# Routed attention into a gated MLP on one core: centroid constants in two PSUM banks, tanh and gate over 512 columns, and a new order

## The chip, the cores and the metric

The program runs on one core of a Trainium2 chip. The core has a matrix engine (PE), whose weight loads are shown apart (PEld), a vector engine (DVE), a scalar engine for activation functions (ACT), a general engine (POOL), and SP, which here issues DMAs. Each engine takes its own instructions in order, and engines wait for each other through semaphores. PE writes to PSUM, which has eight banks of 128 partitions x 512 fp32 values; POOL and DMAs can't reach it. The metric is the device time of one launch in microseconds (us), lower is better.

## The reference

Attention in which a query sees only the keys that have the same nearest centroid, then an MLP with w_in, SiLU and w_out. B, H, S, D = 4, 8, 768, 64; 16 centroids for each head; 3072 tokens, model width 512, hidden width 2048.

```python
q_assign = np.argmax(np.einsum('bhsd,hcd->bhsc', q_n, c_n), axis=-1)   # q_n, k_n, c_n: rows of length 1
k_assign = np.argmax(np.einsum('bhsd,hcd->bhsc', k_n, c_n), axis=-1)
mask = q_assign[:, :, :, None] == k_assign[:, :, None, :]
scores = scale * np.matmul(q, k.transpose(0, 1, 3, 2))
scores = np.where(mask, scores, -1000000000.0)
attn = np.exp(scores - np.max(scores, axis=-1, keepdims=True))
attn = attn / (np.sum(attn, axis=-1, keepdims=True) + 1e-09)
x = np.matmul(attn, v)                        # to [B * S, H * D]
h = x @ w_in
out = (h * (1.0 / (1.0 + np.exp(-h)))) @ w_out
```

## The kernel before

`build` describes the work as a graph of some 1,900 steps. A step has a list of engines that may do it, the steps it comes after, and the buffers that it uses (`POOLS`: so many tiles of a name; `M` are the eight PSUM banks). What sets the order is the string `PLAN`: it holds the buffer number for every buffer, and then the steps in the order in which they are recorded, each with the engine chosen for it. Every engine thus runs its steps in the plan's order. Entries below zero are filler matmuls on zeros (L951), which use PE while it would have nothing to do; there are 43.

The stages, with the letters that end a step's tag:

- **Centroids.** Loaded, scaled to length 1, split in an fp16 high and low part (`c_split`), transposed on PE (`c_turn`, L330) and copied to `st2` (`c_place2`, two steps, one for the high part and one for the low) and `stk` (`c_place`). `st2` holds the constants with which the first batch's logits are made.
- **Tokens of a pair of heads.** A pair p of heads of batch b has one buffer `ab`. For the first 8 of 12 token tiles of batch 0 (`part2`): an fp32 transpose of two tiles at once on PE (L579), a *split* on ACT (`hi`, L594), a *residual* on DVE (`lo`, L599), a *move* of the second tile's half to partitions 0 to 63, and the logits on PE (L624 to 626). For the last 4 tiles of batch 0 (`part`, tags that end in .8, such as p0.3.0.8 for pair 3) and for all tiles of the later batches: a split (L452 to 456) and a residual (L459) first, then a transposing DMA from SP (L517), then logits against `stk` (L529 and 530, or L532).
- **Codes** (`codes`): DVE finds the maximum of 16 logits, marks it and *flips* the marks (L436); four *puts* copy them to partitions 64 to 95 of `ab`, on POOL, DVE or ACT, or as a DMA on SP (L390). So the scores of different clusters fall far below those of equal ones.
- **Attention** (`attention`): scores of 128 x 512 (L685), exponential on ACT to a tile `P` (L688), product with the values (L713; the values are loaded at L257 and *cast* to `vt`), reciprocal and normalisation on DVE, a transpose (L770, in batch 0) and a *settle* to `xt`.
- **MLP** (`mlp`): unit by unit of tokens (`UNITS`: batch 0 has one of 256 tokens and one of 512, the rest have 384). For each of the 16 blocks of hidden width: four up-projections (L801) to a bank, tanh on ACT (L809), gate on DVE (L812), then the down-projections (L828), the copy out and the store. The first L801 needs all four pairs' `xt` for the first 256 tokens and the first weights, which POOL casts.

From the first L801 on, the plan mixes attention of the later batches with the MLP of the earlier ones.

Of the kernel before, what the change touches and what calls it, by code (L numbers as in the profile page):

```python
# [25 lines left out]
    "11543XvaUa;<08X8W*vvspm({+9jHIiazwtnnkkNf5nk&?iyp>(J@a+%_i5zs8%TrcSts4^|Y{weeZ43*}M&!mD2no=3a?r4yn=N*jx(y&wjafjU"
    "2n;uFckmvp8&K5U|(Bnke-4Enr6k{oPB=#GuV_$L?p)?s33mRMbRk*w&duya{%9ll)m~1~F!Tyo^$=#F{*HO&)q#=*7O59YGrf@%A}!W>11<7t+|"
    "7hD_`@X7{wSAv4m;rJxy~Xe&*?+||p$h<Uc+E@<W*WAfg$^(Ee9jl=W8rs~AlxJb4!lW5*2Y<65#Bdx6_VY7Q)#JT3WsM&>(jlGD8&sg(s*UZ<;f"
    "{@u&=b=3b{Ld~%Y_C_jV{Dwbe)c(bH&W|()aGDnop<~^5BT*t*3Z@l8Jb$H!)8yy_IXiTQ<LoZkYM&M?2nDo<L!UMRP2DMJTd02bY<%E!)67&EOt"
    "zO25c4a)+lP{=o-~ZCfMp6XXmW=k1;Fe%`3@N)u4IPklBl{t%TmXI(|gQnf&y2FWzLeYi1iV@t<1rBmUF8=#84l4%=u?G^2uk74z~zRX3eoy@*+*"  # L30
    "poxKGf5%*VYDR3$NZq%nf3A3IovL9wK6U5A{+<QR`#EN<Tw6r~{(M4yZn}Q122I>~wb84t0UJ$Wd-ssNvt#ZZ_2=pOaS`(8oBDm>`e#zW_DB40fq"
    "=g{5kKx9)TgN3-H4rU(9c%KKQ%%o2fU1R{V$Q!tPR^cy4LI6$Myg5><3>h4^Ew^&9JDyN)hvP?|UZVf87Kg`o0R<xp<Yv^`G_d8l`@Xr0%P0=NPp"
    "66SVOYuzT<Ab?SH4|Ig)+UFU#Zv4CB%kd2JgJq-KbLJzVx=)aNc$8GAl5cT6I<iGoalRs?VB*EmFW8P42kdl(<)V8aqI#>ttz%;J9pW@n#ah!T4s"
    "~qRQl%UfBt!uuH0?s|g)W@C<8KEV##-9Og0Qq2r-Nh8HeG6>`ZD2e!H2LK?qs^C+<1~VaTt5SC3+-Txxi-dm4s8rgpglA*^}%tPqR*fmpgHygbS$"
    "KYPS6>YuQOo}Jk6NyXcx!{yI?oWf=n<DI>Jhr4f~)6b9x)y3vXi2K@Y%O_yFF4LofjH!n-gJ4#E(49zK(gP1ujlhi_pZ427Mr0P@2mcn|(f2{}E{"
# [952 lines left out]
```

## Time and profile before

| | us |
|---|---|
| median of 3 runs | 301.54 (300.48 to 303.38) |
| the profiled execution | 301.66 |
| its span, first to last instruction | 299.9 |
| PE busy in it | 291.2 |
| DVE, ACT, POOL busy | 213.9, 222.6, 89.6 |

A line of a profile's group reads: source line, engine, operation, what it writes and reads, shape, count; then busy time and the mean of one in ns; then the engine's idle time just before and what ended it. A line of the timeline reads: start and length in us, engine, line, operation, count, and in brackets the idle time before it. Durations of instructions that follow each other overlap a little. The clock granted to PE is 0.998 of the full one.

### The profile page before, as it was taken

What the parts mean: (1) busy time and instruction counts of PE and PEld (TensorE: products, weight loads), DVE (VectorE), ACT (ScalarE), POOL (GpSimd) and SP (SyncE); (2) the same over time, 40 slices, a digit from 0 to 9 for tenths busy, and PEclk for the clock granted to TensorE, in tenths of its full rate; (3) what the DMA queues carried; (4) which work ended last, traced back from release to release, by engine and by line L of the source; (5) the groups of instructions that cost most, each with busy time, mean ns of one, the idle gap of its engine ahead of it and who ended that gap; (6) DMA issues with size and microseconds to landing.
All of it is one profiled execution on the core that took longest, in us unless ns stands there. A gap on an engine that the chain in (4) does not pass through costs nothing.

```text
span 299.9 us, 7820 instructions
## 1 busy us (share of the span) xinstructions
PE 291.2 (97%) x3044; PEld 187.0 (62%) x3044; DVE 213.9 (71%) x512; ACT 222.6 (74%) x456; POOL 89.6 (30%) x151
## 2 busy tenths in 40 slices
PE   7898999999999999999999999999999999999995
PEld 5776898645555676766656566566665655554553
DVE  5999988878898999889999686676552323465140
ACT  2898999888669898998888867889988732343221
POOL 3787776443655406040833212100200000000000
PEclk9999999999999999999999999999999999999999
...
GB/s 203 263 227 291 218 262 348 116 281 293 249 283 243 232 245 215 224 202 300 124 170 126 134 144 196 149 5 3 66 2 26 28 32 67 0 93 49 1 107 105
DMA packets 83382, 47.42 MB, mean 158 GB/s; under 512 B 60688, under 2 KB 78352, under 8 KB 83344
## 3 DMA queue, kind: packets, MB, share of 16 engines
...
q10 hardware_dynamic: 144, 0.03, 0.1%
...
## 4 chain that ended last, share of the span: by engine, by line
PE 83%; DVE 10%; ACT 2%; issue 2%; DMA 1%; POOL 1%; SPq 0%; DVEq 0%
PE M L801 26%; PE M L828 26%; PE M L685 17%; PE M L713 10%; DVE hl L459 3%; PE M L532 2%; DMA nat<-in_q_dram 1%; DVE gq L812 1%; DVE lo L599 1%; DVE ab L191 1%; DVE ohT L436 1%; POOL ab L191 1%; DVE oh L429 1%; DVE mx L419 1%; DVE M L422 1%
## 5 line engine op out<-in xcount | busy, mean ns | idle before, releaser
L688 ACT ACTIVATE P<-M 128x512 f16<-128x512 f32 x288 | 155.8, 622 | 18.6 <-PE M L685 17.9
L812 DVE SCALAR_TENSOR_TENSOR gq<-tn,M 128x384 f16<-128x384 f32 (+2 forms) x128 | 66.7, 548 | 47.9 <-ACT tn L809 46.4
L801 PE MATMUL M<-xt,win_s 128*128 128x384 f16 (+2 forms) x512 | 95.7, 325 | 0.0
L828 PE MATMUL M<-wout_s,gq 128*128 128x512 f16 (+2 forms) x400 | 94.8, 370 | 0.0
L685 PE MATMUL M<-ab 96*128 96x256 f16 (+1 forms) x432 | 90.5, 308 | 1.4 <-DVE ab L191 0.9
L809 ACT ACTIVATE tn<-M 128x384 f32<-128x384 f32 (+2 forms) x128 | 61.2, 512 | 36.5 <-PE M L801 32.4
L801 PEld LDWEIGHTS <-win_s 128*128 128x128 f16 x512 | 48.7, 97 | 33.5 <-issue 0.2
L828 PEld LDWEIGHTS <-gq 128*128 128x128 f16 x400 | 37.4, 97 | 36.2 <-issue 0.4
L191 POOL COPY ab<-ohT 32x384 f16<-32x384 f16 (+2 forms) x69 | 38.4, 557 | 55.6 <-DVE ohT L436 31.2
L713 PEld LDWEIGHTS <-P 128*128 128x128 f16 x1152 | 45.7, 97 | 10.5 <-issue 0.7
L713 PE MATMUL M<-vt,P 128*128 128x65 f16 x1152 | 49.2, 193 | 0.3 <-DVE oh L429 0.2
L685 PEld LDWEIGHTS <-ab 96*128 96x128 f16 x432 | 38.0, 97 | 18.3 <-DVE ab L191 0.7
L459 DVE SCALAR_TENSOR_TENSOR hl<-nat,hl 128x768 f16<-128x768 f32 (+1 forms) x28 | 29.6, 1073 | 0.1
L191 POOL CAST vt<-nv 128x384 f16<-128x384 f32 x19 | 11.3, 607 | 32.5 <-DMA nv<-in_v_dram 21.3
L456 POOL TENSOR_SCALAR hl<-nat 128x768 f16<-128x768 f32 (+1 forms) x19 | 15.1, 804 | 19.4 <-DMA nat<-in_k_dram 14.2
L436 DVE STREAM_TRANSPOSE ohT<-oh 128x384 f16<-128x384 f16 (+2 forms) x33 | 18.3, 557 | 1.0
L401 DVE TENSOR_REDUCE M<-M 128x192 f32<-128x384 f32 x24 | 13.4, 559 | 6.1 <-PE M L532 4.4
L189 ACT COPY ot<-M 128x512 f32<-128x512 f32 (+2 forms) x14 | 7.8, 558 | 12.0 <-PE M L828 12.0
L191 DVE COPY ot<-M 128x512 f32<-128x512 f32 x11 | 7.6, 687 | 8.9 <-PE M L828 8.9
L429 DVE TENSOR_SCALAR oh<-M 128x96 f16<-128x96 f32 (+4 forms) x62 | 13.1, 252 | 0.7
L743 DVE TENSOR_TENSOR xn<-M,rz 128x384 f16<-128x384 f32 x24 | 13.1, 551 | 0.7 <-DVE rz L732 0.3
L732 DVE RECIPROCAL rz<-M 128x6 f32<-128x6 f32 (+1 forms) x36 | 6.6, 182 | 8.3 <-PE M L713 8.1
...
## 6 DMA issues: line engine op xcount, KB each, us to landing
nv<-in_v_dram SPq DMA_DIRECT2D x16, 384.0 KB, 5.1
...
nat<-in_k_dram SPq DMA_DIRECT2D x15, 384.0 KB, 4.7
nat<-in_q_dram SPq DMA_DIRECT2D x12, 384.0 KB, 4.8
...
```

What stands on the lines that cost most here:

```text
L191: eng(en).tensor_copy(out, in_)
L429: e.nc.vector.tensor_scalar(out=T(oh)[:, 0:n, 0:HC].rearrange("p (g i) c -> p g i c", g=groups)[:, :, i0:i1, :], in0=from_().rearrange("p ...
L436: e.nc.vector.transpose(T(ohT)[:, 0:n, :].rearrange("p n c -> p (n c)"), T(oh)[:, 0:n, :].rearrange("p n c -> p (n c)"))
L456: e.nc.gpsimd.tensor_scalar(out=dh(), in0=src(), scalar1=QS, scalar2=1.0, op0=ALU.mult, op1=ALU.mult)
L459: e.nc.vector.scalar_tensor_tensor(out=dl(), in0=src(), scalar=QS, in1=dh(), op0=ALU.mult, op1=ALU.subtract)
L685: e.nc.tensor.matmul(bank(sb)[:, at : at + 128 * (c - a)], ab[0:96, kt[m], :], q, start=True, stop=True)
L688: e.nc.scalar.activation(out=T(P)[:, 0:n], in_=bank(sb)[:, 0:n], func=AF.Exp, bias=0.0, scale=ESC)
L713: e.nc.tensor.matmul(bank(O)[:, at : at + D + 1], T(P)[:, c : c + 128], T(vb)[:, VW * m : VW * m + D + 1], start=(m == 0), stop=(m == NJ - ...
L801: e.nc.tensor.matmul(bank(bk)[:, 0:n], e.win_s[:, r, ts(fb, 128)], T(X)[:, r, 128 * j0 : 128 * j1], start=(r == 0), stop=(r == NR - 1),)
L809: e.nc.scalar.activation(out=T(tn)[:, 0:n], in_=bank(bk)[:, 0:n], func=AF.Tanh, bias=0.0, scale=1.0)
L812: e.nc.vector.scalar_tensor_tensor(out=gq(fb // 4)[:, fb % 4, 0:n], in0=T(tn)[:, 0:n], scalar=1.0, in1=bank(bk)[:, 0:n], op0=ALU.add, op1= ...
L828: e.nc.tensor.matmul(bank(bk)[:, 0 : c1 - c0], gq(quarter)[:, fc % 4, ts(t, 128)], e.wout_s[:, fc, c0:c1], start=(fc == 0), stop=(fc == NF ...
```

## The change

- `c_turn` does two transposes, one for each part, to two banks (`pcs`), each to partitions 0 to 63. `c_place2` is cut by heads: the first pair's constants of both parts first (`s_pair`, which the first pair's logits wait for), then the other six heads (`s_others`, which the rest waits for).
- In `mlp`, units of 256 tokens put two hidden blocks side by side in one bank, and one tanh and one gate of 512 columns serve both.
- 21 tiles `P` instead of 19; `mx`, `oh` and `ohT` have 16 instead of 24 rows of codes, as none needs more. `EARLY` is gone; it was empty.
- A new `PLAN`: other engines for some steps (18 puts on SP before, 30 now; the moves of batch 0 all on POOL before, now five on POOL, two on ACT and one on SP), and another order on all engines.

```diff
-    pc = buf("M", 64)
+    pcs = [buf("M", 64), buf("M", 64)]
 
     def c_turn(_):
-        e.nc.tensor.transpose(bank16(pc)[:, 0:128], e.chl.rearrange("p a d -> p (a d)"), e.ident)
+        for part, pc in enumerate(pcs):
+            e.nc.tensor.transpose(bank16(pc)[0:64, 0:128], e.chl[:, part, :], e.ident)
...
-    def c_place2(part):
+    def c_place2(part, h0, h1):
...
-                copy(
-                    en, e.st2[64 * s : 64 * s + 64, part, :, HC * s : HC * s + HC],
-                    bank16(pc)[64 * part : 64 * part + 64, 0:128].rearrange("d (h c) -> d h c", c=HC),
-                )
+                copy(en, e.st2[64 * s : 64 * s + 64, part, h0:h1, HC * s : HC * s + HC], turned_c(part)[:, h0:h1])
...
-        s_log = step("PE", logits, after=[s_hi, s_lo, s_cent2], use=[A, lo2, Lb], kind="mm", size=(3 * w, 32), tag=tag + "l", key=key + 1)
+        s_log = step("PE", logits, after=[s_hi, s_lo, s_others if p else s_pair], use=[A, lo2, Lb], kind="mm", size=(3 * w, 32), tag=tag + "l", key=key + 1)
...
-        for fb in range(NFB):
-            bk, tn = buf("M", n), buf("tn")
+        per = 512 // n if n <= 256 else 1
+        for f0 in range(0, NFB, per):
+            bk, tn = buf("M", n * per), buf("tn")
...
             def tanh(_, bk=bk, tn=tn):
-                e.nc.scalar.activation(out=T(tn)[:, 0:n], in_=bank(bk)[:, 0:n], func=AF.Tanh, bias=0.0, scale=1.0)
+                e.nc.scalar.activation(out=T(tn)[:, 0 : n * per], in_=bank(bk)[:, 0 : n * per], func=AF.Tanh, bias=0.0, scale=1.0)
```

What the new plan moves is seen at three places. The first is the start, on ACT, from the first split (L594) to the first exponential (L688). `st2` are the constants, `ab0` is pair 0's buffer, `ohT` the flipped marks. Before:

```order
L594 ACTIVATE ab0_87<-M0_151 128x512
L189 COPY st2_68<-M1_152 64x8x16 x2
L594 ACTIVATE ab0_87<-M2_153 128x512
L594 ACTIVATE ab1_88<-M4_155 128x512
L594 ACTIVATE ab1_88<-M6_157 128x512
L189 COPY ab0_87<-ohT0_140 32x8x32 x3
L189 COPY ab0_87<-ohT1_141 32x8x32
L594 ACTIVATE ab2_89<-M7_158 128x512
L594 ACTIVATE ab2_89<-M0_151 128x512
L688 ACTIVATE P0_102<-M5_156 128x512
```

Now:

```order
L596 ACTIVATE ab0_87<-M0_153 128x512
L188 COPY st2_69<-M1_154 64x2x16 x2
L188 COPY st2_69<-M2_155 64x2x16 x2
L596 ACTIVATE ab0_87<-M3_156 128x512
L188 COPY ab0_87<-ab0_87 64x512
L188 COPY st2_69<-M2_155 64x6x16 x2
L188 COPY st2_69<-M1_154 64x6x16 x2
L596 ACTIVATE ab1_88<-M6_159 128x512
L596 ACTIVATE ab1_88<-M7_160 128x512
L188 COPY ab1_88<-ab1_88 64x512
L188 COPY ab0_87<-ohT0_142 32x8x32
L188 COPY ab0_87<-ohT1_143 32x8x32
```

All constants of `st2` are ACT's now, and two moves; the two splits into `ab2` (a third pair) moved behind the first exponential, and two of four puts to POOL. On DVE at the same place, from the split of p0.0.0.8 on, before:

```order
L454 TENSOR_SCALAR hl0_82<-nat0_76 128x8x64
L191 COPY st2_68<-M1_152 64x8x16 x2
L599 SCALAR_TENSOR_TENSOR lo20_85<-M0_151,ab0_87 128x512
L459 SCALAR_TENSOR_TENSOR hl0_82<-nat0_76,hl0_82 128x8x64
L419 TENSOR_REDUCE mx0_135<-M3_154 128x8
```

Now:

```order
L456 TENSOR_SCALAR hl0_82<-nat0_76 128x8x64
L461 SCALAR_TENSOR_TENSOR hl0_82<-nat0_76,hl0_82 128x8x64
L601 SCALAR_TENSOR_TENSOR lo20_85<-M0_153,ab0_87 128x512
L601 SCALAR_TENSOR_TENSOR lo21_86<-M3_156,ab0_87 128x512
L421 TENSOR_REDUCE mx0_137<-M4_157 128x8
```

The two constant copies left DVE, and the residual into `hl0` (what the transposing DMA reads) moved ahead of the one into `lo20` (what the first logits read).

The second place is SP's queue between the transposing DMA of p0.1.0.8 (to `ab2`) and that of batch 1's second part (to `ab4`). `nv` are values, `gq` the landing place of weights. Before:

```order
L517 DMA_TRANSPOSE ab2_89<-hl2_84 128x8x128
L257 DMA nv1_81<-in_v_dram 128x2x384
L257 DMA nv0_80<-in_v_dram 128x2x384
L282 DMA gq1_122<-in_moe_w_in_dram 128x4x256
L517 DMA_TRANSPOSE ab1_88<-hl1_83 128x8x128
L282 DMA gq2_123<-in_moe_w_in_dram 128x4x256
L517 DMA_TRANSPOSE ab4_91<-hl0_82 128x12x128
L282 DMA gq3_124<-in_moe_w_in_dram 128x4x256
L282 DMA gq4_125<-in_moe_w_in_dram 128x4x256
```

Now:

```order
L519 DMA_TRANSPOSE ab2_89<-hl0_82 128x8x128
L281 DMA gq0_123<-in_moe_w_in_dram 128x4x256
L392 DMA ab3_90<-ohT1_143 32x16x32
L519 DMA_TRANSPOSE ab1_88<-hl2_84 128x8x128
L256 DMA nv1_81<-in_v_dram 128x2x384
L281 DMA gq1_124<-in_moe_w_in_dram 128x4x256
L281 DMA gq2_125<-in_moe_w_in_dram 128x4x256
L519 DMA_TRANSPOSE ab4_91<-hl1_83 128x12x128
L281 DMA gq3_126<-in_moe_w_in_dram 128x4x256
```

The values of pair 2 (the second `nv` before, the only one now) and the weights moved behind the transposing DMA of p0.3.0.8 (to `ab1`), and a put came into the queue ahead of it. What that DMA waits for is DVE's residual into its `hl`. On DVE before it, before:

```order
L436 STREAM_TRANSPOSE ohT1_141<-oh0_138 128x256
L436 STREAM_TRANSPOSE ohT0_140<-oh1_139 128x512
L191 COPY ab3_90<-ohT0_140 32x16x32 x4
L459 SCALAR_TENSOR_TENSOR hl1_83<-nat1_77,hl1_83 128x8x64
L459 SCALAR_TENSOR_TENSOR hl0_82<-nat0_76,hl0_82 128x12x64
```

Now:

```order
L438 STREAM_TRANSPOSE ohT1_143<-oh0_140 128x512
L461 SCALAR_TENSOR_TENSOR hl2_84<-nat1_77,hl2_84 128x8x64
L438 STREAM_TRANSPOSE ohT0_142<-oh1_141 128x256
L190 COPY ab3_90<-ohT1_143 32x16x32
L190 COPY ab3_90<-ohT0_142 32x8x32
L190 COPY ab3_90<-ohT1_143 32x16x32 x2
```

The residual of p0.3.0.8 (the one of 128x8x64) moved ahead of a flip and of the puts into `ab3`.

The third place is ACT where the 256-token unit begins. Before:

```order
L809 ACTIVATE tn0_142<-M5_156 128x256
L688 ACTIVATE P2_104<-M4_155 128x512
L809 ACTIVATE tn1_143<-M6_157 128x256
L809 ACTIVATE tn2_144<-M7_158 128x256
L688 ACTIVATE P3_105<-M1_152 128x512
```

Now:

```order
L813 ACTIVATE tn0_144<-M6_159 128x512
L813 ACTIVATE tn1_145<-M4_157 128x512
L690 ACTIVATE P14_116<-M2_155 128x512
L690 ACTIVATE P7_109<-M7_160 128x512
L690 ACTIVATE P8_110<-M5_158 128x512
```

One tanh now stands where two stood, with exponentials moved between them.

More of the change, by code (lines that the diff above doesn't have):

```diff
@@ L26 @@
[L26 to L35, printed above, removed]
@@ L91 @@
 PAIRED = 6
-EARLY = {}
 CHUNK = 8
@@ L102 @@
     "vt": (10, [128, 6 * 72], f16),
-    "P": (19, [128, 512], f16),
+    "P": (21, [128, 512], f16),
     "gq": (8, [128, 2048], f16),
@@ L106 @@
     "xn": (3, [128, 6, 128], f16),
-    "mx": (3, [128, 24], f32),
-    "oh": (2, [128, 24, 32], f16),
-    "ohT": (2, [128, 24, 32], f16),
+    "mx": (3, [128, 16], f32),
+    "oh": (2, [128, 16, 32], f16),
+    "ohT": (2, [128, 16, 32], f16),
     "tn": (3, [128, 512], f32),
@@ L355, in build @@
     s = step("POOL", c_root, after=[s, s_ident], kind="const", size=520, tag="croot")
[L356 to L361 removed]
+    s = step("DVE", c_split, after=[s], kind="const", size=950, tag="csplit")
+    s = step("PE", c_turn, after=[s, s_ident], use=pcs, kind="mm", size=(2, 128), tag="cturn")
+    s_pair = [
+        step("DVE ACT", c_place2(part, 0, 2), after=[s, s_const2], use=[pcs[part]], kind="place2", size=300, tag="cplace2")
+        for part in range(2)
+    ]
+    s_others = [
+        step("DVE ACT", c_place2(part, 2, H), after=[s, s_pair[part]], use=[pcs[part]], kind="place2", size=430, tag="cplace3")
+        for part in range(2)
+    ]
+    s_cent = step("DVE", c_place, after=[s, s_const, s_others], use=pcs, kind="const", size=690, tag="cplace")
     abuf, ready = {}, {}
@@ L812, in gate @@
+            def gate(_, f0=f0, bk=bk, tn=tn):
                 e.nc.vector.scalar_tensor_tensor(
-                    out=gq(fb // 4)[:, fb % 4, 0:n], in0=T(tn)[:, 0:n], scalar=1.0, in1=bank(bk)[:, 0:n],
-                    op0=ALU.add, op1=ALU.mult,
-                )
-            y = step("ACT", tanh, after=[s], use=[bk, tn], kind="T", size=n, tag=tag + "T", key=key + fb)
-            gates.append(step("DVE", gate, after=[s, y], use=[bk, tn, g4], kind="G", size=n, tag=tag + "G", key=key + fb))
+                    out=gq(f0 // 4)[:, f0 % 4 : f0 % 4 + per, 0:n], in0=T(tn)[:, 0 : n * per].rearrange("p (f c) -> p f c", c=n),
+                    scalar=1.0, in1=bank(bk)[:, 0 : n * per].rearrange("p (f c) -> p f c", c=n), op0=ALU.add, op1=ALU.mult,
+                )
@@ L819, in mlp @@
+            y = step("ACT", tanh, after=ups, use=[bk, tn], kind="T", size=n * per, tag=tag + "T", key=key + f0)
+            s = step("DVE", gate, after=[ups, y], use=[bk, tn, g4], kind="G", size=n * per, tag=tag + "G", key=key + f0)
+            gates.extend([s] * per)
         for t in range(j1 - j0):
@@ L926 @@
     e.wout_s = const.tile([128, NFB, DM], f16, name="wout_s")
+    e.half = const.tile([128, 1], f32, name="half")
     e.ident = const.tile([128, 128], f16, name="ident")
@@ L930 @@
     e.st2 = const.tile([128, 2, H, 2 * HC], f16, name="st2")
-    e.half = const.tile([128, 1], f32, name="half")
     e.zeros = const.tile([128, 256], f16, name="zeros")
```

137 lines of the change are left out of this document (70 added, 67 removed).

## The prediction

> **What bounds the kernel now.** I read the page first: the busy shares, then the chain.
>
> ```profile
> span 299.9 us, 7820 instructions
> PE 291.2 (97%) x3044; PEld 187.0 (62%) x3044; DVE 213.9 (71%) x512; ACT 222.6 (74%) x456; POOL 89.6 (30%) x151
> ...
> PE 83%; DVE 10%; ACT 2%; issue 2%; DMA 1%; POOL 1%; SPq 0%; DVEq 0%
> ```
>
> PE is the bound: 97% busy and 83% of the chain. DVE and ACT are busy 71 and 74% and hold little of the chain. So the question is where PE is not busy. Busy time by stretch answers it (columns: length, then busy time of PE, PEld, DVE, ACT, POOL, clock, DMA share, GB/s).
>
> ```profile
> 0.00:10.00 10.00, 7.97 (x65) 5.96 (x66) 6.45 (x22) 3.60 (x6) 3.85 (x23) 1.00 0.73 218
> 10.00:20.00 10.00, 9.11 (x135) 8.00 (x134) 9.58 (x27) 9.67 (x20) 8.17 (x19) 1.00 1.04 266
> 20.00:30.00 10.00, 8.42 (x156) 7.16 (x152) 9.84 (x25) 9.17 (x20) 7.92 (x14) 1.00 1.09 254
> 30.00:40.00 10.00, 9.72 (x173) 8.55 (x173) 9.42 (x34) 9.75 (x21) 7.50 (x10) 1.00 1.03 245
> 40.00:50.00 10.00, 10.00 (x155) 8.98 (x154) 8.46 (x27) 10.00 (x27) 6.71 (x11) 1.00 1.15 296
> 50.00:60.00 10.00, 9.43 (x129) 7.27 (x127) 8.24 (x22) 9.16 (x21) 5.70 (x7) 1.00 0.57 167
> 100.00:150.00 50.00, 50.00 (x600) 32.77 (x599) 45.88 (x108) 45.75 (x94) 17.77 (x26) 1.00 0.96 220
> 290.00:300.00 10.00, 6.80 (x45) 3.70 (x43) 0.69 (x1) 1.30 (x3) 0.00 (x0) 0.95 0.26 96
> ```
>
> PE idles 2.03, 0.89, 1.58 and 0.28 us in the four stretches up to 40, 0.57 us at 50 to 60, and 3.1 us at the end, where the last output tile is copied and stored. Between 100 and 150 it idles not at all. Up to 40 DVE is at 94 to 98% from 10 on and ACT at 92 to 98%: they feed PE. From the first up-projection on, PE has MLP work for every hole:
>
> ```profile
> 37.82 0.46 PE L532 MATMUL M<-stk,ab 128*128 128x32 f16 x12
> 38.63 1.47 PE L801 MATMUL M<-xt,win_s 128*128 128x256 f16 x12
> L951 PE MATMUL M<-zeros 128*128 128x256 f16 x43 | 7.9, 327 | 1.1 <-DVE zeros L196 1.1
> ```
>
> So a gain has to make the first L801 come before 38.63, or close the 0.57 us hole. All PE idle before 60 is 5.35 us, and the 43 filler matmuls (L951) are 7.9 us of busy time that is no work; both plans hold 43 of them. More than some 5 us isn't there to be won.
>
> **The change part by part.** The sum is made against the profiled execution, 301.66 us (span 299.9 and 1.8 around it), 0.12 above the median of 301.54.
>
> *Centroid constants (start).* Rows of the start, then groups kept apart by shape:
>
> ```profile
> 6.67 0.44 DVE L191 COPY st<-M 64x128 f16<-64x128 f16 x2
> 7.13 0.69 DVE L599 SCALAR_TENSOR_TENSOR lo<-M,ab 128x512 f16<-128x512 f32 x1
> 7.20 0.53 ACT L189 COPY st<-M 64x128 f16<-64x128 f16 x2 [1.49 <-DVE st L191]
> 8.45 1.33 SPq L517 DMA_TRANSPOSE ab<-hl  x1
> 12.53 1.08 ACT L594 ACTIVATE ab<-M 128x512 f16<-128x512 f32 x2
> 13.50 2.09 ACT L688 ACTIVATE P<-M 128x512 f16<-128x512 f32 x4
> ```
>
> ACT waits 1.49 us for DVE's half of the constants, and DVE, whose next work follows at once (7.13), spends 0.44 us on them. Now ACT does all eight copies (four of 2 heads, four of 6 heads) from two banks. At most 8 x 0.265 = 2.1 us (each like the 64x128 copy); a small copy is not free, so I take 1.7. ACT has 6.4 us idle in the first 10, which hides them and the two moves of 64x512 that it also takes over (estimated at 0.6 us each, since a 512-column ACTIVATE of the row at 12.53 takes 0.54). DVE loses 0.44 us. The second transpose is one matmul more in a place of fillers (7.9 / 43 = 0.18 us each): 0 to 0.2 us, and I take 0. The residual of p0.0.0.8 now stands ahead of the one of p0.0.0.0 on DVE: the transposing DMA (8.45) is issued about 1 us earlier, and the first logits end about 0.3 us later (0.69 more, 0.44 less ahead of their residual), which eats part of the 0.44. The first exponential, at 13.50 behind two splits (12.53, 1.08 us), comes to about 12.4, because those two splits now stand behind it; that is an exchange on ACT, worth 0.1 us.
>
> *Up to the first up-projection.* The settle that releases L801 is DVE's. Ahead of it DVE now has two constant copies, one cast, one flip of 256 and two puts of 512 columns fewer, and two splits (512 and 768 columns) more:
>
> ```profile
> L191 DVE CAST vt<-nv 128x384 f16<-128x384 f32 x11 | 4.4, 402 | 0.0
> L436 DVE STREAM_TRANSPOSE ohT<-oh 128x256 f16<-128x256 f16 x6 | 2.6, 438 | 0.2
> L191 DVE COPY ab<-ohT 32x512 f16<-32x512 f16 x6 | 3.0, 502 | 0.1
> L454 DVE TENSOR_SCALAR hl<-nat 128x512 f16<-128x512 f32 x1 | 0.8, 845 | 0.5 <-DMA nat<-in_q_dram 0.5
> L454 DVE TENSOR_SCALAR hl<-nat 128x768 f16<-128x768 f32 x7 | 4.4, 644 | 0.7 <-DMA nat<-in_k_dram 0.6
> 16.43 12.04 ACT L688 ACTIVATE P<-M 128x512 f16<-128x512 f32 x24
> 29.30 3.54 ACT L688 ACTIVATE P<-M 128x512 f16<-128x512 f32 x7 [0.83 <-PE M L685]
> ```
>
> -0.44 - 0.40 - 0.44 - 1.00 + 0.85 + 0.64 = -0.8 us. ACT, with 48 exponentials ahead of the first tanh instead of 47 and the same four splits since the first scores, allows between -0.1 us (its hole of 0.83 stays) and -0.9 (it closes). I take DVE's 0.8, as DVE is the fuller one. The twelve logits at 37.82 (0.46 us with the last one's drain, which overlaps; I take 0.3) stood ahead of the first L801 and now stand behind it, so 0.5 us of PE time is won: **-0.5**, bounds -0.9 (no logits to make up for) and +0.3 (the first logits' delay comes through and nothing else).
>
> *Tanh and gate of 512 columns.*
>
> ```profile
> 39.77 0.55 ACT L809 ACTIVATE tn<-M 128x256 f32<-128x256 f32 x1
> 40.04 0.78 ACT L688 ACTIVATE P<-M 128x512 f16<-128x512 f32 x1
> L812 DVE SCALAR_TENSOR_TENSOR gq<-tn,M 128x512 f16<-128x512 f32 x16 | 10.3, 673 | 2.2 <-ACT tn L809 2.2
> L812 DVE SCALAR_TENSOR_TENSOR gq<-tn,M 128x256 f16<-128x256 f32 x16 | 6.4, 414 | 1.7 <-ACT tn L809 1.3 <-issue 0.2
> ```
>
> The next ACTIVATE starts 0.27 us after a 256-column tanh, and 512 columns follow each other every 12.04 / 24 = 0.50 us: 16 x 0.27 - 8 x 0.50 = 0.3 us off ACT. DVE saves 16 x 0.414 - 8 x 0.673 = 1.2 us. But PE is 10.00 of 10.00 busy at 40 to 50, where these stand: its own backlog hides both, **0**; were that cover gone, ACT's 0.3 would count. The Trainium skill, "ScalarE: Activation LUTs" (What ACT_TABLE_LOAD costs), gives 186 ns + 0.833 ns a column with about 93 ns of overlap, so an estimate from that page is 8 x 92 ns = 0.7 us; the trace's 0.3 is less. If ACT set the end there, the sum would be 300.2 by the page and 300.6 by the trace.
>
> *The hole at 56.*
>
> ```profile
> 53.60 1.83 DVE L459 SCALAR_TENSOR_TENSOR hl<-nat,hl 128x768 f16<-128x768 f32 x1
> 53.59 2.75 POOL L191 CAST wout_s<-gq 128x1024 f16<-128x1024 f32 x2
> L459 DVE SCALAR_TENSOR_TENSOR hl<-nat,hl 128x768 f16<-128x768 f32 x24 | 26.7, 1129 | 0.1
> 56.05 0.28 PE L770 MATMUL M<-ident,xn 128*128 128x128 f16 x2 [0.57 <-DVE xn L737]
> ```
>
> PE waits 0.57 us for a normalisation that DVE does behind a residual of 1.83 us, 0.7 over its mean. With DVE ahead by some 0.8 + 1.2 us I let half of it go: **-0.3**, bounds -0.6 and +0.6 (another such place). The Trainium skill, "SBUF — State Buffer" (Who interferes with whom), says that a VectorE instruction with two SBUF inputs contends with a GpSimd one that reads SBUF; the two rows above overlap and agree. By that rule the residual is stretched again wherever a POOL copy runs beside it, the hole stays, and the sum is 301.2.
>
> *Two more P tiles, smaller mx and oh:* **0**. Of the exponentials' idle time 17.9 of 18.6 us is put down to scores, and none of the rest shown to a reader of P.
>
> ```profile
> L688 ACT ACTIVATE P<-M 128x512 f16<-128x512 f32 x288 | 155.8, 622 | 18.6 <-PE M L685 17.9
> ```
>
> *Twelve more puts on SP* (30 for 18), one move on SP, other casts: **0** where PE has work, bounds 0 and +3; the upper end is the third rival. *The last 10 us*: the same split of the last tile, **0**.
>
> Sum: 301.66 - 0.5 - 0.3 = 300.9; less the 0.12 to the median, **300.8 us**.
>
> **The rivals.**
>
> *More comes through.* If the 1.1 us by which the exponentials start earlier last until the first up-projection, the gates' 1.2 us count and the 0.57 us hole closes, 301.54 - 2.9 = 298.6. For it: DVE at 9.84 of 10 from 20 to 30. Against it: ACT still has the two splits to do, and PE hides the gates.
>
> *It is hidden or given back*, 301.5: ACT, not DVE, paces the front (9.75 of 10 at 30 to 40), with no fewer exponentials to do, and a POOL copy stretches the residual at the hole again. Against it: DVE is as full, and the order behind the hole is another.
>
> *SP holds the values and weights up* (slower). SP issues its DMAs in the program's order:
>
> ```profile
> 22.68 1.71 SPq L257 DMA_DIRECT2D nv<-in_v_dram  x2
> 29.48 1.23 SPq L517 DMA_TRANSPOSE ab<-hl  x1
> nv<-in_v_dram SPq DMA_DIRECT2D x16, 384.0 KB, 5.1
> 35.14 0.35 DVE L191 CAST vt<-nv 128x384 f16<-128x384 f32 x1
> ```
>
> Before, the values of pair 2 were issued ahead of the transposing DMA of p0.3.0.8, which SP could issue only at 29.48, when DVE had its residual. Now they and two weight loads stand behind it. That residual moved ahead of a flip and four puts on DVE (0.44 + 4 x 0.50 = 2.4 us; the constants and the cast that went, 0.84, and the split that came, 0.85, are even), so it should be ready near 29.48 - 2.4 = 27.1. DVE would reach its cast of these values (35.14) 0.8 us earlier, at 34.3; with 1.23 us for the transposing DMA's issue, 0.85 for the values' own and 5.1 to land, the transposing DMA must start by 27.1. So there is no slack, and what it is late by, DVE waits. If it stays at 29.48, the values land at 36.7 and the first L801, 3.5 us behind the cast before, comes at 40.2; POOL, which casts the same values ahead of three puts and the first weight blocks (1.4 us each by the row at 53.59), gives PE its second pair of blocks near 42. Some 3 us late: 304.7.
>
> **How the numbers follow.** Forecast 300.8: 0.53. Hidden, 301.5: 0.20. More comes through, 298.6: 0.12. SP, 304.7: 0.15. The range 298.5 to 303.8 takes in the first two with their bounds, the third's centre and the milder half of the fourth (values a little late), and leaves out about 0.15. One per cent, 3 us, is about what a measurement of this kernel can tell from no change. Faster by over 1% (under 298.5) takes half of the third case and the tails of the first two, 0.10; slower (over 304.6) half of the fourth and stalls not foreseen, 0.10; within 1%, 0.80.
>
> **What would show it.** Right: the first exponential near 12.4, no wait of ACT for DVE's constants, the transposing DMA of p0.3.0.8 issued before 28, the first up-projection near 37.8, PE at 10.00 of 10.00 from 60 on. Wrong: PE idle past 60 in the stages of the later batches, where the new order could run DVE or SP late and where I count nothing; the values' cast on DVE waiting for DMA; the first exponential early but the first up-projection no earlier (then ACT paces).

## The result, and the profile after

| | before | changed kernel |
|---|---|---|
| median, runs beside each other | 301.5 (300.48 to 304.0, 22 runs) | 303.8 (300.79 to 306.18, 22 runs) |
| ratio to before | | 1.0061, 95% interval 1.0040 to 1.0081 |
| the profiled execution, its span | 301.66, 299.9 | 301.85, 300.1 |

The change made the kernel slower, by 0.6% or 1.8 us as a ratio and 2.3 us between the medians. The profiled execution of the changed kernel is one of its quickest: it ran at a mean granted clock of 1.00, while 12 of the 20 executions behind the ratio, which leaves out the two slowest, had 0.989 to 0.994 (median 304.1; the other eight 302.7), so the profile shows less than the median loses.

The page of the changed kernel, its span, busy times and chain:

```profile
span 300.1 us, 7835 instructions
PE 290.9 (97%) x3045; PEld 186.9 (62%) x3045; DVE 205.5 (68%) x487; ACT 226.9 (76%) x462; POOL 83.3 (28%) x145
...
PE 82%; DMA 8%; ACT 6%; DVE 1%; SPq 1%; issue 1%; POOL 0%; ACTq 0%; POOLq 0%
```

PE is the bound as before. But DMA holds 8% of the chain where it held 1%, ACT 6% where it held 2%, and DVE 1% where it held 10%: more of what PE waits for now are transfers. The stretches of the changed kernel that differ (columns as in the prediction):

```profile
20.00:30.00 10.00, 7.23 (x156) 6.35 (x152) 7.83 (x24) 8.01 (x17) 4.89 (x9) 1.00 1.04 201
30.00:40.00 10.00, 9.90 (x169) 8.87 (x168) 8.46 (x28) 10.00 (x22) 7.83 (x12) 1.00 1.31 269
50.00:60.00 10.00, 10.00 (x135) 7.57 (x133) 8.83 (x20) 9.27 (x21) 5.12 (x7) 1.00 0.67 195
100.00:150.00 50.00, 49.06 (x580) 31.47 (x578) 42.47 (x103) 43.36 (x90) 18.19 (x29) 1.00 0.96 217
```

PE idles 2.77 us from 20 to 30 (1.58 before), 0.10 from 30 to 40 (0.28), nothing at 50 to 60 (0.57) and 0.94 from 100 to 150, where it had not idled at all. The rows of the changed kernel behind these:

```profile
12.00 1.08 ACT L690 ACTIVATE P<-M 128x512 f16<-128x512 f32 x2
27.20 0.60 PE L687 MATMUL M<-ab 96*128 96x256 f16 x4 [2.60 <-DMA ab<-ohT]
38.34 0.60 PE L803 MATMUL M<-xt,win_s 128*128 128x256 f16 x4
38.78 0.45 PE L534 MATMUL M<-stk,ab 128*128 128x32 f16 x12
39.08 1.47 PE L803 MATMUL M<-xt,win_s 128*128 128x256 f16 x12
107.88 0.46 PE L534 MATMUL M<-stk,ab 128*128 128x32 f16 x12 [0.86 <-ACT P L690]
...
PEld L534 <- DMA ab<-hl: 1.4, 1, 1.4
```

The last line is of the waits between 100 and 112: who waits for what, us in total, times, longest. The first exponential starts 1.5 us earlier than in the kernel before (12.00 in place of 13.50). That lead is gone at 27.20: the scores of pair 1 wait 2.6 us for one put (`ab<-ohT`) that the new plan gave to SP. The first up-projection (L803) comes at 38.34, against 38.63. But the fifth, ahead of which both kernels have done the twelve logits, comes at 39.08 against 39.06: nothing is won there. At 107.88 the row names an exponential as what ended last, but PE's weight load for the same matmuls waited 1.4 us for a transposing DMA (`ab<-hl`).

The put of p0.1.1.0c on SP's queue, in the changed kernel:

```profile
20.11 0.57 SPq L256 DMA_DIRECT2D nv<-in_v_dram  x1
20.72 0.47 SPq L239 DMA_DIRECT2D nat<-in_q_dram  x1
21.36 0.59 SPq L392 DMA_DIRECT2D ab<-ohT  x1
```

Its flip was done at 17.80. Each DMA's landing, from the same trace:

```
values, 384 KB   issued 20.11   landed 25.86
q,      384 KB   issued 20.72   landed 26.86
put,     32 KB   issued 21.36   landed 27.07
```

The put lands 5.7 us after its issue but 0.2 us after the load ahead of it. In the whole trace 165 DMAs were issued by SP, and no one landed ahead of one issued earlier.

### The profile page after: what moved, and what is told of

Same layout as the page of the kernel before. It is cut to its first block, busy times and chain, and to the rows that moved or that the text cites. A ratio compares the mean times of both kernels' runs of the same rounds, so it can differ in the third digit from the quotient of the medians.

```text
span 300.1 us, 7835 instructions
## 1 busy us (share of the span) xinstructions
PE 290.9 (97%) x3045; PEld 186.9 (62%) x3045; DVE 205.5 (68%) x487; ACT 226.9 (76%) x462; POOL 83.3 (28%) x145
## 4 chain that ended last, share of the span: by engine, by line
PE 82%; DMA 8%; ACT 6%; DVE 1%; SPq 1%; issue 1%; POOL 0%; ACTq 0%; POOLq 0%
PE M L803 26%; PE M L833 25%; PE M L687 17%; PE M L715 10%; ACT P L690 5%; DMA ab<-hl 4%; PE M L534 2%; DMA ab<-ohT 2%; DMA nat<-in_k_dram 1%; ACT ab L596 1%; SPq L239 1%; PE M L772 1%; POOL ab L190 0%; ACT ot L188 0%; DVE mx L421 0%
## 5 line engine op out<-in xcount | busy, mean ns | idle before, releaser
L803 PE MATMUL M<-xt,win_s 128*128 128x384 f16 (+2 forms) x512 | 95.4, 325 | 0.0
L833 PE MATMUL M<-wout_s,gq 128*128 128x512 f16 (+2 forms) x400 | 93.5, 370 | 0.0
L816 DVE SCALAR_TENSOR_TENSOR gq<-tn,M 128x384 f16<-128x384 f32 (+1 forms) x120 | 65.6, 575 | 36.4 <-ACT tn L813 35.7
L813 ACT ACTIVATE tn<-M 128x384 f32<-128x384 f32 (+1 forms) x120 | 59.0, 524 | 30.0 <-PE M L803 24.5
L803 PEld LDWEIGHTS <-win_s 128*128 128x128 f16 x512 | 48.8, 97 | 32.0 <-issue 0.2
L190 POOL COPY ab<-ohT 32x384 f16<-32x384 f16 (+2 forms) x70 | 41.9, 602 | 56.8 <-DVE ohT L438 20.5
L715 PE MATMUL M<-vt,P 128*128 128x65 f16 x1152 | 49.9, 193 | 0.0
L461 DVE SCALAR_TENSOR_TENSOR hl<-nat,hl 128x768 f16<-128x768 f32 (+1 forms) x28 | 27.1, 971 | 0.2
L458 POOL TENSOR_SCALAR hl<-nat 128x768 f16<-128x768 f32 (+1 forms) x16 | 13.6, 859 | 13.7 <-DMA nat<-in_q_dram 5.8
```

Of the source, the lines that this page charges most:

```text
L190: eng(en).tensor_copy(out, in_)
L458: e.nc.gpsimd.tensor_scalar(out=dh(), in0=src(), scalar1=QS, scalar2=1.0, op0=ALU.mult, op1=ALU.mult)
L461: e.nc.vector.scalar_tensor_tensor(out=dl(), in0=src(), scalar=QS, in1=dh(), op0=ALU.mult, op1=ALU.subtract)
L715: e.nc.tensor.matmul(bank(O)[:, at : at + D + 1], T(P)[:, c : c + 128], T(vb)[:, VW * m : VW * m + D + 1], start=(m == 0), stop=(m == NJ - ...
L803: e.nc.tensor.matmul(bank(bk)[:, c0 : c0 + n], e.win_s[:, r, ts(fb, 128)], T(X)[:, r, 128 * j0 : 128 * j1], start=(r == 0), stop=(r == NR ...
L813: e.nc.scalar.activation(out=T(tn)[:, 0 : n * per], in_=bank(bk)[:, 0 : n * per], func=AF.Tanh, bias=0.0, scale=1.0)
```

## The experiments

Each is the changed kernel (unless it says before) with a few entries of its plan altered after decoding. An entry is a step and its engine; for a put 0 is POOL, 1 DVE, 3 SP. `move(a, b)` takes entry a out and sets it in at b. Ratios are to the kernel before, run beside it.

| run | edit | median (runs) | ratio, 95% interval |
|---|---|---|---|
| changed kernel | | 303.8 (22) | 1.0061, 1.0040 to 1.0081 |
| e1 | one front put to DVE | 304.79 (5) | 1.0104, 1.0077 to 1.0132 |
| e4 | that put on SP ahead of two loads | 307.48 (6) | 1.0187, 1.0152 to 1.0222 |
| e5 | two front puts off SP | 303.0 (10) | 1.0052, 1.0018 to 1.0086 |
| e6 | e5, a q load behind a transposing DMA | 303.4 (10) | 1.0055, 1.0022 to 1.0089 |
| e7 | e6, a values load behind another | 303.75 (5) | 1.0070, 1.0019 to 1.0120 |
| e2 | 12 more fillers in the front's wait | 303.25 (10) | 1.0052, 1.0024 to 1.0080 |
| e3 | before, one front put to SP | 302.09 (12) | 1.0018, 0.9999 to 1.0038 |
| e11 | tanh and gate apart again | 303.93 (12) | 1.0060, 1.0034 to 1.0087 |
| e8 | e5, 25 later puts to POOL | 301.68 (10) | 1.0012, 0.9990 to 1.0033 |
| e9 | 25 later puts to POOL alone | 301.83 (12) | 0.9998, 0.9973 to 1.0023 |
| e10 | e8 and 14 fillers | 301.32 (12) | 0.9975, 0.9953 to 0.9997 |
| e12 | e9 and e2 | 302.08 (12) | 1.0024, 0.9997 to 1.0052 |
| e13 | four of the 25 to POOL | 300.56 (12) | 0.9986, 0.9960 to 1.0012 |
| e14 | the other 21 to POOL | 302.92 (12) | 1.0054, 1.0031 to 1.0076 |
| e18 | two of the four to POOL | 302.36 (12) | 1.0042, 1.0020 to 1.0064 |
| e15 | before, its later puts as after | 305.9 (6) | 1.0153, 1.0121 to 1.0185 |
| e16 | before, no later put on SP | 301.32 (12) | 0.9994, 0.9972 to 1.0016 |
| e17 | e13, e5 and 14 fillers | 301.24 (12) | 1.0002, 0.9978 to 1.0027 |

### The wait at 27.2: e1, e4, e5, e6, e7, e3

The first theory was the plainest: the 2.6 us wait is the loss.

e1:

```diff
+    order[2 * 176 + 1] = 1
```

> One put of p0.1.1.0c (pair 1's centroid rows) goes back from SP to DVE, at the same place of the order; nothing else changes. Theory P (the put on SP is what the change lost): scores of pair 1 no longer start at 27.20 but near 25, the 2.6 us wait of PE there falls under 0.6 us, the median falls by 2.0 to 4.5 us against the changed kernel's 303.8 (the upper end if the runs at a granted clock of 0.994 go as well). Theory C (the loss is the lower clock alone, and it comes from another place than this wait, such as the 0.86 us at 107.9): the wait goes and the median falls by at most 2.3 us, with most runs still at 0.994. Rival M (the wait is slack of PE that later work makes up for): the wait goes, the median stays within 0.7 us of 303.8.

None of the three held. The wait of 2.6 us went (the scores start at 25.10), and the median rose by 1 us. PE's timeline in e1, and its stretches of 4 us:

```profile
31.12 0.81 PE L687 MATMUL M<-ab 96*128 96x256 f16 x6 [2.00 <-DVE xn L739]
...
32.14 1.28 PE L687 MATMUL M<-ab 96*128 96x256 f16 x6
```

```profile
28.00:32.00 4.00, 2.00 (x42) 1.65 (x39) 2.72 (x10) 1.86 (x4) 1.56 (x4) 1.00 1.24 216
32.00:36.00 4.00, 4.00 (x55) 3.46 (x52) 1.98 (x6) 3.40 (x8) 2.32 (x4) 0.57 1.42 308
```

The wait moved to the scores of pair 2 at 31.12. The row names a normalisation, but that was long done; pair 2's own put on SP landed at 31.03, behind a weight load of 512 KB that landed at 29.53. And after a stretch with PE busy 2.00 of 4.00 us, the granted clock is 0.57 in the next: six matmuls take 1.28 us that took 0.81 just before. All five executions had a mean clock of 0.994 or less.

e4:

```diff
+    move(151, 176)
+    move(160, 176)
```

> The put of p0.1.1.0c stays on SP, but the loads of values and of q that were issued ahead of it (20.11 and 20.72) are issued behind it. Theory Q (a put is late because the queue lands its transfers in the order of issue, behind 384 KB loads): it is issued near 20.1 and lands near 22.2, right behind the three puts ahead of it; the wait of PE at 27.2 goes as in the run with the put on DVE, and the two loads land 0.2 to 0.7 us later. Rival S (an SP put of a centroid row takes some 5.7 us by itself): it lands near 25.8 and PE still waits 1 us or more.

The put, issued at 21.69, landed at 24.10, 2.4 us later in place of 5.7, and the scores started at 24.63 with no wait: theory Q. What moved behind it paid: the transposing DMA of p0.1.0.8 landed at 28.51 (28.08 in the changed kernel; PE waited 2.14 us) and pair 2's put at 31.60 (30.00 there; 1.79 us), and the clock stood at 0.50 from 32 to 36. It is the slowest of all.

e5 and e6, in the front's whole queue:

```diff
+    order[2 * 176 + 1] = 1
+    order[2 * 201 + 1] = 0
```

> The put of p0.1.1.0c goes to DVE as in the first run, and the next SP put of the same stage, of p0.2.1.0c (pair 2), goes to POOL. Theory F (the queue lands in the order of issue; each small put behind a 384 or 512 KB load costs PE the wait for that load, and the wait only moves to the next such put when one is taken away): the 2.0 us wait of PE at 31.1, where the scores of pair 2 stood behind a weight load that landed at 29.5, goes as well; PE idles under 3 us between 20 and 40 in place of 5.4, its clock stays at 1.00 there, and the median is 300 to 302. Rival G (the front is set by ACT or DVE, and the waits of PE are where their lateness shows): PE's idle time from 20 to 40 stays above 4.5 us under other names, and the median stays above 303.

```diff
+    order[2 * 176 + 1] = 1
+    order[2 * 201 + 1] = 0
+    move(161, 178)
```

> As the run with two puts off SP, and the second q load of the later pair (issued at 21.11, ahead of the transposing DMA of p0.1.0.8) is issued behind that DMA. Theory F: the transposing DMA lands near 25.9 to 26.5 instead of 27.7, the 0.86 us wait of PE for it at 27.7 goes, and the median falls by a further 0.3 to 1.2 us. Rival G: the wait goes, the median stays within 0.4 us of the run with two puts off SP.

Both named waits went, and the next stood elsewhere, in e5 and in e6:

```profile
39.41 0.47 PE L534 MATMUL M<-stk,ab 128*128 128x32 f16 x12 [2.18 <-DMA ab<-hl]
```

```profile
35.84 0.53 PE L715 MATMUL M<-vt,P 128*128 128x65 f16 x12 [3.19 <-POOL vt L190]
```

In e5 it is a transposing DMA, in e6 the values of pair 2, which landed at 35.04 (32.16 in the changed kernel). The medians are 0.4 to 0.8 us under 303.8, which the intervals don't tell from nothing. So theory F is right that transfers land in the order of issue, a small one behind the large one ahead, and wrong on the price: each cure hands the wait to another transfer of the same queue.

e7 adds to e6's edits:

```diff
+    move(794, 795)
```

> As the run before in this list, and at 100 us the load of values that stands ahead of the transposing DMA of p2.0.1.0 is issued behind it. Theory F: that DMA lands about 1.1 us earlier than 107.8, PE's wait of 0.9 to 1.4 us for it near 108 goes, and the median falls by a further 0.6 to 1.2 us. Rival H (PE has a backlog there or loses the time at the next such DMA): the wait goes or moves to the next transposing DMA, and the median stays within 0.4 us.

Rival H held. The transposing DMA was issued at 101.40 and landed at 106.09, PE did not wait for it, and then it waited for later ones, 0.8 us at 110.9 and 0.6 at 131.0 (e5: 0.7 at 110.8, e6: 0.4 at 112.9).

e3, the kernel before with one such put on SP:

```diff
+    order[2 * 172 + 1] = 3
```

> The kernel before with one of the two POOL puts of p0.1.1.0c moved to SP at the same place of the order, behind a load of 384 KB and ahead of the weight load. Theory P: it is issued near 20.7 and lands behind that load near 25.3; the scores of pair 1, at 24.59 before, come near 25.4 to 26, 0.8 to 1.5 us later, and the median rises by 0.5 to 2 us. Rival M (slack): the scores come later and the median stays within 0.4 us of the kernel before.

The scores of pair 1 came at 25.45 in place of 24.59, as theory P said, and the median rose by 0.4 us. The interval of the ratio allows 0 to 1.1 us, so what these 0.9 us cost stays open.

### The lower clock: e2, e10, e12

```diff
+    order[2 * 197 + 1] = 15
```

> The changed kernel with 15 instead of 3 zero matmuls ahead of the scores of pair 1, 12 more at 0.18 us each: they fill 2.2 us of the 2.6 us that PE waits there, while the put stays on SP and the wait's end stays at 27.2. Theory C1 (PE's idle time in this wait lowers its granted clock for a while in most runs): the runs at 0.994 go, and the median falls by 1.5 to 1.8 us to about 302.2. Rival C2 (the lower clock has nothing to do with this wait): most runs stay at 0.994 and the median stays within 0.5 us of 303.8.

The fillers in e2, and the scores behind them:

```profile
24.28 1.80 PE L957 MATMUL M<-zeros 128*128 128x256 f16 x15
26.55 0.60 PE L687 MATMUL M<-ab 96*128 96x256 f16 x4 [0.47 <-DMA ab<-ohT]
```

All ten executions had a mean clock of 0.999 or 1.00: that bears out C1, which has PE's idle time there take the clock down. But the median fell by 0.55 us (0.3 by the ratios), not 1.5 to 1.8; the executions at full clock still spread from 301.07 to 304.50. So the clock in the front is not the main loss.

e10 and e12 ask the same with the later puts gone (`late` are the 25 entries of e9, below; -5 is a filler on the bank that the next logits use):

```diff
+    order[2 * 176 + 1] = 1
+    order[2 * 201 + 1] = 0
+    for i in late:
+        order[2 * i + 1] = 0
+    order[2 * 214 : 2 * 214] = array("h", [-5, 14])
```

> Two front puts and the 25 later ones off SP, as in the run with the late puts off, and 14 zero matmuls ahead of the logits that wait for the transposing DMA of p0.1.0.8, 0.11 us each, so that PE is busy for 1.5 us of a wait of up to 1.8. Theory C1 (a wait of some 2 us by PE brings half the clock for 2 to 4 us): the runs at 0.993 go, all stay at 0.999 or 1.0, and the median falls by 0.5 to 1.3 us below 301.7, to or below the kernel before. Rival C2 (the low clock costs nothing there, since ACT and DVE set the front): the clock rises, the median stays within 0.4 us of 301.7.

```diff
+    for i in late:
+        order[2 * i + 1] = 0
+    order[2 * 197 + 1] = 15
```

> The changed kernel with its 25 later puts on POOL, and 15 zero matmuls instead of 3 ahead of the scores of pair 1, whose put stays on SP. Theories C1 and L together: all runs at 0.999 or 1.0, the wait between 24 and 27 stays, and the median is 301.3 to 302.2, that is 0.5 us or more below the run with the late puts moved alone. Rival: as that run, within 0.3 us.

In e10 all twelve executions kept 0.999 or more (six of ten in e8 were at 0.994 or less) and the median is 0.4 us under e8's. By the ratios it is 1.1 us (1.0012 and 0.9975), since the kernel before ran at 301.22 beside e8 and at 301.75 beside e10. In e12 four of twelve still fell to 0.994, and neither the median nor the ratio is under e9's. Within one kernel the executions at the lower clock are longer, by 1.4 us in the changed kernel and by 2.2 in e13, but by the ratios fillers gave 0.3 us in e2, 1.1 in e10 and nothing in e12. What the lower clock costs by itself stays open.

### The gates: e11

```diff
-                e.nc.scalar.activation(out=T(tn)[:, 0 : n * per], in_=bank(bk)[:, 0 : n * per], func=AF.Tanh, bias=0.0, scale=1.0)
+                for j in range(per):
+                    e.nc.scalar.activation(
+                        out=T(tn)[:, j * n : (j + 1) * n], in_=bank(bk)[:, j * n : (j + 1) * n], func=AF.Tanh, bias=0.0, scale=1.0
+                    )
```

and the gate likewise.

> The changed kernel with the eight tanh and eight gates of 512 columns done as two of 256 columns each, in the same steps. The prediction's term (hidden by PE's backlog): PE stays at 10.00 of 10.00 from 40 to 60, median within 0.5 us of 303.8. Rival (the gates pace the stretch): PE idles 0.5 us or more between 40 and 60 and the median rises by 0.5 to 1.5 us.

The stretches of e11:

```profile
40.00:50.00 10.00, 10.00 (x156) 8.98 (x154) 9.19 (x28) 10.00 (x26) 5.07 (x8) 1.00 1.07 361
50.00:60.00 10.00, 10.00 (x132) 7.42 (x131) 8.98 (x23) 9.52 (x23) 5.11 (x7) 1.00 0.50 134
```

PE stays full, and the median is that of the changed kernel: hidden.

### The later puts: e8, e9, e13, e14, e18

e8 has e5's two edits and the 25 puts on SP from 97 us on set to POOL; e9 has the 25 alone:

```diff
+    late = [758, 766, 830, 853, 937, 1085, 1086, 1108, 1148, 1183, 1212, 1239, 1240,
+            1257, 1305, 1342, 1350, 1352, 1369, 1468, 1498, 1527, 1531, 1543, 1544]
+    for i in late:
+        order[2 * i + 1] = 0
```

> As the run with two puts off SP, and the 25 later puts that stand on SP (batches 1 to 3, from 97 us on) go to POOL. Theory F says nothing is gained unless PE waits behind one of them: PE's waits past 60 us in the changed kernel are 1.4 us, and its wait for a transposing DMA at 107.9 has no put ahead of it on SP that is not landed: median within 0.7 us of the run with two puts off. Rival K (the thirty puts on SP as such, by the time that SP spends on issuing them, delay the later loads): the median falls by 1 us or more against that run.

> The changed kernel with its 25 later puts (from 97 us on) on POOL instead of SP; the puts of the front stay on SP. Theory L (what is left of the loss beside the front is PE behind late puts and behind transposing DMAs that stand behind them on SP, 1 to 1.5 us in an ordinary execution): the front wait near 27 stays, PE's waits between 100 and 150 fall from 1.4 to 2.3 us to under 0.8, and the median falls by 0.8 to 1.5 us against the changed kernel's 303.8. Rival N (the gain of the run with all later puts off was chance): the median stays within 0.4 us of 303.8.

Here was the loss. e9 is 2.0 us under the changed kernel and level with the kernel before, though its front still has the wait (1.9 us for the put) and seven of its twelve executions the lower clock. From 100 to 150 its PE is busy 49.92 of 50.00. Theory F's "nothing is gained" was wrong, and the fall that rival K named came (1.3 us from e5 to e8). That SP's issue time is the reason, these two runs don't show; e13's rows bear on it.

e13, then e14 (the other 21), then e18:

```diff
+    for i in [758, 766, 830, 853]:
+        order[2 * i + 1] = 0
```

```diff
+    for i in late[4:]:
+        order[2 * i + 1] = 0
```

```diff
+    for i in [758, 766]:
+        order[2 * i + 1] = 0
```

> The changed kernel with only the first four of its 25 later puts on POOL instead of SP: those that SP issues between 97 and 112 us, each taking 0.6 us of its time, ahead of two transposing DMAs. Theory L1 (a put costs by SP's issue time, and by the transfers that are issued later behind it): the transposing DMA that PE waits for at 107.9 is issued 1.2 us earlier, PE's wait there falls from 1.0 to under 0.4 us, and the median falls by 0.6 to 1.2 us from 303.8. Rival L2 (the loss is in the other 21): median within 0.4 us of 303.8.

> The complement: the other 21 later puts on POOL, the four of 97 to 112 us kept on SP. Theory L1: PE's wait of about 1.0 us at 107.9 stays, the waits between 118 and 135 (0.3 to 1.1 us in the looks so far) go, and the median falls by 0.6 to 1.2 us; this run's fall and that of the run with four puts off add up to about 2.0, the fall with all 25 off. Rival L2: nearly the whole 2.0 us comes here.

> The changed kernel with two of the four puts on POOL: those of p1.3.1.0 and p1.3.0.0 that SP issues at 97.2 and 97.9, ahead of the transposing DMA of p2.0.1.0; the two of p2.1.0.0 at 107.4 and 111.3 stay on SP. Theory L1 (SP's issue time ahead of that transposing DMA is what PE waits for): the DMA is issued near 99.8 instead of 101.1 and lands near 106.6, PE's wait at 107.9 falls under 0.4 us, and the median falls by 1.2 us or more from 303.8, most of the 3.2 that the four gave. Rival L3 (the two later ones do it, by holding back the transposing DMAs for which PE waits between 118 and 135): the wait at 107.9 goes, the median stays above 302.8.

Four puts do it: e13 is 3.2 us under the changed kernel between the medians, 2.3 us (0.75%) by the ratios, more than L1's 0.6 to 1.2. The other 21 give 0.9 or 0.2 us, within the intervals. The clock isn't behind it: among the executions at 0.998 or more the changed kernel's median is 302.7 and e13's 300.3. SP's queue in the changed kernel, from the first two of the four to the transposing DMA that PE waits for at 107.88:

```profile
97.21 1.33 SPq L392 DMA_DIRECT2D ab<-ohT  x2
98.59 1.31 SPq L762 DMA_TRANSPOSE xt<-xn  x1
99.95 0.58 SPq L239 DMA_DIRECT2D nat<-in_q_dram  x1
100.57 0.46 SPq L256 DMA_DIRECT2D nv<-in_v_dram  x1
101.14 2.39 SPq L519 DMA_TRANSPOSE ab<-hl  x1
```

and in e13:

```profile
96.76 1.24 SPq L762 DMA_TRANSPOSE xt<-xn  x1
98.05 0.58 SPq L239 DMA_DIRECT2D nat<-in_q_dram  x1
98.67 0.47 SPq L256 DMA_DIRECT2D nv<-in_v_dram  x1
99.24 2.45 SPq L519 DMA_TRANSPOSE ab<-hl  x1
...
100.00:150.00 50.00, 50.00 (x588) 32.43 (x586) 43.21 (x106) 44.34 (x93) 18.54 (x32) 1.00 0.96 218
```

In the changed kernel SP issues without a rest: between 97 and 112 its issues take 14.0 of the 15 us, with no pause over 0.11 us between two. In e13 they take 13.2, and SP pauses for 0.4 and 0.9 us. The two puts (1.33 us) stand ahead of the DMA for which PE waits. It is issued at 101.14, 1.9 us later than in e13, and lands at 107.84, 3.2 us later. So the puts' issue time is 1.3 of these 3.2 us; as much again arises between issue and landing (6.7 us in place of 5.4), and these rows don't say why. PE's wait is gone in e13, and from 100 to 150 it is busy 50.00 of 50.00.

The other profiles agree in direction. From 100 to 150 PE idles 0.4 to 1.9 us in the eight kernels that keep all 25 later puts on SP (the changed one, e1, e2, e4 to e7, e11), and 0 to 0.3 in e8, e9, e10, e12 and e13; e17 has 0.98. So idle time of PE there is some 1 us of the 2.3. Where the rest lies, one profile of each kernel doesn't show.

e18, with two of the four moved, is 1.4 us under the changed kernel between the medians, as L1 said, but only 0.6 by the ratios. The transposing DMA was issued at 102.04, not near 99.8, in an execution that had run at half the clock from 25.9 to 32.7. PE didn't wait for it, but it waited elsewhere in the same stretch:

```profile
111.83 0.47 PE L534 MATMUL M<-stk,ab 128*128 128x32 f16 x12 [0.54 <-DMA ab<-hl]
...
131.78 0.47 PE L534 MATMUL M<-stk,ab 128*128 128x32 f16 x12 [0.62 <-DMA ab<-hl]
```

So the two behind seem to share in it; how the loss is split among the four, the ratios (1.0061, 1.0042, 0.9986) don't settle.

### The same in the old order, and a faster version: e15, e16, e17

e15 gives the kernel before, in its own order, the changed kernel's share of later puts on SP (16 to SP, 6 from SP to POOL); e16 takes its 15 off:

```diff
+    for i in [709, 897, 904, 1020, 1048, 1103, 1151, 1243, 1293, 1329, 1356, 1396, 1438, 1464, 1504, 1587]:
+        order[2 * i + 1] = 3
+    for i in [704, 794, 895, 1024, 1041, 1047]:
+        order[2 * i + 1] = 0
```

```diff
+    for i in [704, 782, 794, 895, 978, 1024, 1041, 1047, 1058, 1234, 1254, 1343, 1400, 1582, 1590]:
+        order[2 * i + 1] = 0
```

> The kernel before with the puts of its batches 1 to 3 handed out as in the changed kernel: 25 on SP in place of 15, for the same units as there (16 go from POOL, DVE and ACT to SP, 6 from SP to POOL); its front and its order stay. Theory L: PE waits 0.5 to 2 us more between 85 and 150, where it waited 0.5, and the median rises by 0.7 to 2 us. Rival O (it is the new order of steps around the puts, not their engine): the median stays within 0.4 us of the kernel before.

> The kernel before with its 15 later puts on SP moved to POOL; front and order stay. Theory L: PE's waits between 60 and 150, 0.76 us in its profile, fall, and the median falls by 0.2 to 0.7 us against the kernel before. Rival P2 (POOL's puts, in line behind its casts and moves, are late as well): the median stays or rises.

e15 lost 4.3 us, more than theory L gave it. SP's queue in e15, PE's wait, and SP's waits from 95 to 145:

```profile
125.61 3.16 SPq L517 DMA_TRANSPOSE ab<-hl  x1
132.19 0.61 SPq L390 DMA_DIRECT2D ab<-ohT  x1
132.85 1.11 SPq L240 DMA_DIRECT2D nat<-in_k_dram  x2
134.01 1.25 SPq L390 DMA_DIRECT2D ab<-ohT  x2
135.31 2.92 SPq L517 DMA_TRANSPOSE ab<-hl  x1
...
141.30 0.50 PE L532 MATMUL M<-stk,ab 128*128 128x32 f16 x12 [3.20 <-DMA ab<-hl]
...
SPq L390 <- DVE ohT L436: 6.5, 2, 3.4
```

This is the other way in which a put on SP costs: SP stood still for 3.4 us at a put whose flip DVE had not made, with two loads, two more puts and a transposing DMA queued behind. That DMA landed at 141.25, and PE waited 3.2 us for it. So it is the puts' engine, and not the new order alone, that loses time. But the old plan's 15 cost nothing that e16 can show: its ratio is 0.9994, though the interval leaves room for theory L's 0.2 to 0.7 us. These runs show no price of a put on SP as such, only one that depends on what stands behind it.

e17 has e13's four, e5's two and e10's fillers:

```diff
+    order[2 * 176 + 1] = 1
+    order[2 * 201 + 1] = 0
+    for i in [758, 766, 830, 853]:
+        order[2 * i + 1] = 0
+    order[2 * 214 : 2 * 214] = array("h", [-5, 14])
```

> The changed kernel with the four puts of 97 to 112 us on POOL, the two front puts of pairs 1 and 2 on DVE and POOL, and 14 zero matmuls ahead of the logits of p0.1.0.8. Theories L1 and C1: no wait of PE over 0.4 us between 100 and 112, all runs at 0.999 or 1.0, median 299.8 to 300.5, below the 300.56 of the run with four puts off and below the kernel before. Rival (the front's waits only move, and the fillers cost what they save): median 300.5 to 301.5, as the run with all later puts off and the front cleaned (301.32).

The rival held: the front cleaned on top of the four puts gave nothing (301.24 against 300.56, ratios 1.0002 and 0.9986). The two lowest ratios are e10's, whose interval ends just below 1 (0.9953 to 0.9997), and e13's, the lowest median of all, whose interval does not (0.9960 to 1.0012). Among eighteen intervals, one that just clears 1 is weak evidence of a faster kernel.

## Why the prediction was wrong

**The step that failed** is "Twelve more puts on SP (30 for 18), one move on SP, other casts: 0 where PE has work, bounds 0 and +3". It was sized by PE's backlog, and past 60 it was given nothing because PE had been 50.00 of 50.00 busy there. What the runs showed in its place: four of those puts, at 97 to 112, cost 2.3 us by the ratios, and what the traces show of it is PE waiting for the transposing DMAs behind them. A full PE is no proof of slack. SP's issues already took 13.7 of the 15 us from 97 to 112 in the kernel before, and of its ten transposing DMAs that landed between 82 and 138 for logits, one landed 0.04 us and another 0.34 us before PE loaded its weights (the others 0.6 to 3.6). The first of the two, and PE's wait for it between 100 and 140, in the kernel before:

```profile
106.82 1.56 SPq L517 DMA_TRANSPOSE ab<-hl  x1
...
111.90 0.46 PE L532 MATMUL M<-stk,ab 128*128 128x32 f16 x12
...
PEld L532 <- DMA ab<-hl: 0.2, 1, 0.2
```

The text named this as what would make it wrong ("PE idle past 60 in the stages of the later batches"), and gave it no price.

**The third rival**, SP, came nearest in mechanism (transfers late for what stands ahead of them on SP) and had the wrong place. Its values of pair 2 were on time: the transposing DMA of p0.3.0.8 was issued at 26.68, before the 27.1 that decided, and the values landed at 32.16. The place in the front where it did happen, the put of p0.1.1.0c, was not seen, though its move to SP could be read from the plan.

**The start** went as forecast (the first exponential at 12.00 for "near 12.4", no wait for DVE's constants, and ACT's eight copies took 0.75 and 0.96 us, the 1.7 of the sum). **The first up-projection** did not: −0.5 was forecast, and it came 0.3 us earlier, but the fifth, behind the logits, not at all. The wait at 27.2 lies in between, and that it took the lead back is likely, not shown: e13, with 1.9 us of wait there, had the first at 37.71 and the fifth at 38.45, 0.6 us earlier than the kernel before. And e5, e6 and e17 don't gain by taking the puts off that queue: in their profiles PE still idles 2.4 to 3.7 us from 20 to 40 (1.86 before).

**Tanh and gate, 0**: right (e11). **The last 10 us, 0**: right, PE is busy 6.86 of the last 10.2 us, 6.80 of 10.0 before. **Two more P tiles**: not tried alone.

**The hole at 56**: −0.3 was forecast, and all 0.57 us went. The Trainium skill's rule, "SBUF — State Buffer" (Who interferes with whom), was right on the stretch and not on the end. The residual there, with POOL beside it, in the changed kernel:

```profile
53.48 1.45 DVE L461 SCALAR_TENSOR_TENSOR hl<-nat,hl 128x768 f16<-128x768 f32 x1
...
53.11 1.02 POOL L458 TENSOR_SCALAR hl<-nat 128x768 f16<-128x768 f32 x1
```

It takes 1.45 us, above its mean of 1.02 for this shape, so the rule agrees; but PE had other work all that time (10.00 of 10.00). Which of the changes gave PE that work isn't shown, so that the term came out better than forecast is luck in part.

Without the four puts the sum isn't contradicted, nor shown. By its ratio e13 gains 0.4 us, with an interval from 1.2 us gained to 0.4 lost; at 0.998 of the clock or more its executions have a median of 300.3 against 301.4 for the kernel before, −1.2 us where the terms say −0.8.
